# Order and spacing of the weight casts, and earlier splits and turns of two head pairs, in an attention and MLP kernel

## The chip, the cores and the metric

The kernel runs on one core of a Trainium2 chip. The metric is the device time of one execution in microseconds (us). The engines are named as the profile names them: PE is TensorE (PEld its weight loads), DVE is VectorE, ACT is ScalarE, POOL is GpSimd, SP is SyncE, which here only issues transfers. PEclk is the TensorE clock that was granted, as a share of full speed (in the row of slices, in tenths). "L247" is line 247 of the kernel.

## The reference

Eight batches of eight heads, 576 tokens by 64 columns each, go through an attention with a sharp threshold. The result x, 4608 tokens by 512, goes through two layers with h - tanh(h) between them.

```python
scores = scale * np.matmul(q, k.transpose(0, 1, 3, 2))
thresh = np.max(scores, axis=-1, keepdims=True) - tau
scores = np.where(scores >= thresh, scores, -1000000000.0)
scores = scores - np.max(scores, axis=-1, keepdims=True)
attn = np.exp(scores)
attn = attn / (np.sum(attn, axis=-1, keepdims=True) + 1e-09)
attn_out = np.matmul(attn, v)
...
h = x @ w_in            # 512 -> 2048
g = h - np.tanh(h)
return g @ w_out        # 2048 -> 512
```

Inputs and output are float32; q and k are cut on chip into a high and a low float16 part, so that the threshold falls where the reference has it.

## The kernel before

Heads go in pairs: 32 pairs p, four to a batch, nine query tiles to a pair. The program is one loop over *slots* s, one query tile each. In slot s it emits the scores of tile s+8, the shifted and bent scores z of tile s+5, the exponentials of tile s and the product with v of tile s-2. Pair p is therefore first touched in slot 9p - 8. What a pair needs ahead of that is put into slots by a plan: loads 16 to 14 slots before, the splits 8 and 7 before, and the *turns*, which transpose k and q.

```python
    PREP = (
        (LDK, lambda p: load(p, "k")),          # LDK = 16
        (LDK - 1, lambda p: load(p, "q")),
        (LDK - 2, lambda p: load(p, "v")),
        (8, lambda p: split(p, "k")),
        (7, lambda p: split(p, "q")),
        (5, lambda p: turn(p, "k")),
        (4, split_v),
    )
    plan = {}
    for p in range(1, NPAIR):
        first = TPP * p - AHEAD                 # 9 * p - 8
        for d, f in PREP[3 if p == 1 else 0 :]:
            d -= p == 1 and d in (3, 5)
            if d in (7, 8) and q_by_dma(p):
                d = d + 2
            if d == 5 and p >= 5:
                d = 6 if p % 2 else 3
            plan.setdefault(first - d, []).append(lambda p=p, f=f: f(p))
        d = 7 if q_by_dma(p) else 3 - (p == 1 or p % 2 == 0 or p >= 5)
        plan.setdefault(first - d, []).append(lambda p=p: turn(p, "q"))
```

A split is three GpSimd instructions. A turn is nine transposing matmuls on TensorE and a copy by VectorE; but for odd pairs from pair 9 on (and for pair 30), q is turned by one DMA transpose, issued from SP:

```python
    def q_by_dma(p):
        return p >= 2 * HPAIR and (p % 2 == 1 or p == 30)      # HPAIR = 4

    def turn(p, t):
        hl = hls.pop((p, t))
        if t == "q" and q_by_dma(p):
            m = mats[p, t] = qk_pool.tile([P, W], FP16, name=f"{t}T", tag=t)
            nc.sync.dma_start_transpose(                        # L247
                out=m.rearrange("p (c r) -> p c r", c=TPP),
                in_=hl.rearrange("p c a d -> p (c a d)"),
            )
            return
        ...
```

The tiles z of pairs 6 and up are also transposed by DMA from SP (L370), two tiles at a time, five slots before the exponential (L399) reads them. All loads go through SP too (L145 to L153 for q, k and v; L634 and L638 for weights), so one queue carries loads and both kinds of transposes in program order.

The weights of the two layers come in 16 pieces of 512 KB. Each is loaded as float32 into one of two staging buffers and cast to bfloat16 by GpSimd. Every slot in a list casts the piece loaded last and loads the next:

```python
    w_when = [4 * i + 3 for i in range(17)]
    ...
            if s + AHEAD in w_when:
                if loaded:
                    w_cast()            # GpSimd, L626
                piece = next(pieces, None)
                if piece:
                    w_load(piece)       # SP
```

The layers of batch b run in the slots of batch b+1. Batch 0 has none to run beside its attention: it is the *ramp*.

## Time and profile before

| | before |
|---|---|
| median of 3 runs | 533.77 us (532.88 to 534.11) |
| TensorE busy | 505.7 us, 95% of a span of 532.5 us |
| ScalarE, VectorE, GpSimd busy | 82%, 80%, 55% |
| first matmul of the hidden layer | 70.54 us after the start |

A line of a timeline gives the start and the duration in us, the engine, the line and operation, what it writes and reads, and in brackets how long its engine stood idle before it and who ended that. Here are two lines from much later, ScalarE's timeline in batch 1.

```profile
120.95 1.16 ACT L399 ACTIVATE pT<-zT 128x1152 f16<-128x1152 bf16 x1 [0.50 <-DMA zT<-z]
...
124.43 1.16 ACT L399 ACTIVATE pT<-zT 128x1152 f16<-128x1152 bf16 x1 [0.98 <-DMA zT<-z]
```

Both exponentials wait for a transposed z. They are the only waits of that kind worth naming in these 10 us, and together they are 1.5 us. So a DMA, not an engine, is already what arrives last at this place.

### The profile page before, as it was taken

What the parts mean: (1) busy time and instruction counts of PE and PEld (TensorE: products, weight loads), DVE (VectorE), ACT (ScalarE), POOL (GpSimd) and SP (SyncE); (2) the same over time, 40 slices, a digit from 0 to 9 for tenths busy, and PEclk for the clock granted to TensorE, in tenths of its full rate; (3) what the DMA queues carried; (4) which work ended last, traced back from release to release, by engine and by line L of the source; (5) the groups of instructions that cost most, each with busy time, mean ns of one, the idle gap of its engine ahead of it and who ended that gap; (6) DMA issues with size and microseconds to landing.
All of it is one profiled execution on the core that took longest, in us unless ns stands there. A gap on an engine that the chain in (4) does not pass through costs nothing.

```text
span 532.5 us, 12733 instructions
## 1 busy us (share of the span) xinstructions
PE 505.7 (95%) x4584; PEld 289.0 (54%) x4651; DVE 424.0 (80%) x1184; ACT 436.0 (82%) x617; POOL 290.3 (55%) x390
## 2 busy tenths in 40 slices
PE   7988899999999999999999999999999999999997
PEld 3666566555556555555555555656555555444444
DVE  5888878998988998898889898899889887554440
ACT  5999899998898998989888989898899899543330
POOL 7999987784745757475737474575747530000000
PEclk9999999999999999999999999999999999999999
DMA  6654556998997899899997989899989985301113
GB/s 199 188 185 148 160 173 179 207 154 192 180 194 150 186 178 214 169 174 202 179 198 142 211 173 201 155 189 187 205 170 178 197 156 110 105 21 40 39 41 79
DMA packets 202686, 85.31 MB, mean 160 GB/s; under 512 B 170240, under 2 KB 195072, under 8 KB 202624
## 3 DMA queue, kind: packets, MB, share of 16 engines
q1 hardware_dynamic: 202032, 84.08, 74.5%
q8 instruction: 36, 0.59, 0.5%
q10 hardware_dynamic: 592, 0.43, 0.3%
q14 instruction: 26, 0.21, 0.1%
HBM read 36.70 MB, written 9.44 MB: 87 GB/s over the span
## 4 chain that ended last, share of the span: by engine, by line
PE 62%; ACT 11%; POOL 9%; DVE 8%; issue 5%; DMA 4%; SPq 0%; POOLq 0%; ACTq 0%; DVEq 0%
PE psY L519 20%; PE psH L493 16%; PE psS L326 13%; ACT z L363 5%; DMA zT<-z 3%; PE psO L427 3%; ACT pT L399 3%; PE psHt L493 3%; DVE sc L336 3%; POOL kS L264 2%; ACT th L506 2%; DVE g L512 2%; PE ps_k L235 2%; PE psS L317 2%; POOL w_in_sb L626 1%
## 5 line engine op out<-in xcount | busy, mean ns | idle before, releaser
L336 DVE TENSOR_SCALAR_CACHE_REDUCE sc<-psS 128x576 f32<-128x576 f32 x288 | 214.3, 753 | 36.8 <-PE psS L326 22.8
L363 ACT ACTIVATE z<-sc,nb 128x576 bf16<-128x576 f32 x288 | 216.6, 770 | 29.2 <-DVE nb L348 27.1
L519 PE MATMUL psY<-w_out_sb,g 128*128 128x512 bf16 (+1 forms) x571 | 141.7, 373 | 2.4 <-issue 0.8
L264 POOL COPY kS<-kT 64x1152 f16<-64x1152 f16 x62 | 70.9, 1144 | 123.6 <-DVE nb L348 122.0
L399 ACT ACTIVATE pT<-zT 128x1152 f16<-128x1152 bf16 x117 | 135.0, 1154 | 3.7 <-DMA zT<-z 3.7
L493 PE MATMUL psH<-xT,w_in_sb 128*128 128x512 bf16 x436 | 114.1, 379 | 4.3 <-DVE g L512 2.3
L326 PE MATMUL psS<-kT,qT 128*128 128x512 f16 (+1 forms) x512 | 104.4, 285 | 4.6 <-DVE sc L336 2.1
L326 PEld LDWEIGHTS <-qT 128*128 128x128 f16 x1024 | 74.4, 97 | 59.9 <-issue 6.4
L512 DVE SCALAR_TENSOR_TENSOR g<-th,psH 128x512 bf16<-128x512 f32 x128 | 87.5, 684 | 20.4 <-ACT th L506 20.0
L326 PE MATMUL psS<-kS,qT 128*128 128x512 f16 x496 | 101.4, 286 | 0.3 <-POOL kS L264 0.3
L506 ACT ACTIVATE th<-psH 128x512 f32<-128x512 f32 x128 | 74.8, 584 | 23.4 <-PE psH L493 22.8
L519 PEld LDWEIGHTS <-g 128*128 128x128 bf16 x592 | 51.0, 98 | 56.8 <-issue 2.4
L493 PEld LDWEIGHTS <-w_in_sb 128*128 128x128 bf16 x576 | 49.1, 98 | 57.0 <-issue 4.7
L427 PE MATMUL psO<-vb,pT 128*128 128x65 bf16 x1024 | 53.3, 194 | 0.0
L427 PEld LDWEIGHTS <-pT 128*128 128x128 f16 x1024 | 44.2, 98 | 9.4
L188 POOL TENSOR_TENSOR qhl<-qraw,qhl 128x576 f16<-128x576 f32 x31 | 39.7, 1282 | 2.6
L188 POOL TENSOR_TENSOR khl<-kraw,khl 128x576 f16<-128x576 f32 x31 | 39.7, 1281 | 2.6
L391 ACT ACTIVATE pT<-psZ 128x512 f16<-128x512 bf16 (+1 forms) x54 | 35.1, 653 | 5.4 <-PE psZ L382 5.2
L532 DVE COPY yo<-psY 128x512 f32<-128x512 f32 (+1 forms) x31 | 21.1, 682 | 14.0 <-PE psY L519 12.4
L420 PE MATMUL psO<-vb,pT 128*128 128x130 bf16 x128 | 28.3, 221 | 1.8 <-ACT pT L399 1.1
L453 DVE TENSOR_TENSOR osb<-psO,rc 128x256 bf16<-128x256 f32 x64 | 27.2, 424 | 2.2
L258 DVE COPY kT<-ps_k 128x1152 f16<-128x1152 f16 x31 | 23.3, 752 | 5.8 <-PE ps_k L235 5.8
(79 smaller groups left out, 517.3 us busy)
## 6 DMA issues: line engine op xcount, KB each, us to landing
vraw<-in_v_dram SPq DMA_DIRECT2D x32, 256.0 KB, 3.9
out_dram<-yo SPq DMA_DIRECT2D x32, 256.0 KB, 3.1
kraw<-in_k_dram SPq DMA_DIRECT2D x31, 256.0 KB, 3.6
qraw<-in_q_dram SPq DMA_DIRECT2D x31, 256.0 KB, 3.7
wt<-in_moe_w_in_dram SPq DMA_DIRECT2D x8, 512.0 KB, 4.4
wt<-in_moe_w_out_dram SPq DMA_DIRECT2D x8, 512.0 KB, 4.3
zT<-z SPq DMA_TRANSPOSE x117, 3.5
kraw<-in_k_dram SPq DMA_DIRECT2D x32, 32.0 KB, 3.3
```

The costliest lines, as they stand in the source:

```text
L188: nc.gpsimd.tensor_tensor(out=hl[:, :, 1, :], in0=x, in1=hl[:, :, 0, :], op=ALU.subtract)
L264: nc.gpsimd.tensor_copy(out=o, in_=i)
L326: nc.tensor.matmul(out=ps[:, dst], lhsT=lhs, rhs=kk[:, src], start=(n == 0), stop=(n == 1),)
L336: nc.vector.tensor_scalar(out=sc, in0=ps[:, lo : lo + S], scalar1=SC, scalar2=None, op0=ALU.mult, op1=ALU.max, accum_out=mx[:, c : c + 1],)
L363: nc.scalar.activation(out=z, in_=sc, func=ACT.Prelu, bias=nb, scale=1.0, alpha=STEEP)
L391: nc.scalar.activation(out=pt[:, off * P : (off + n) * P], in_=ps[:, 0 : n * P], func=ACT.Exp)
L399: nc.scalar.activation(out=pt[:, 0 : n * P], in_=zts.pop(i)[:, 0:n, :], func=ACT.Exp)
L427: nc.tensor.matmul(out=po[:, t - 1 + ab, :], lhsT=pt[:, blk * P : (blk + 1) * P], rhs=vb[:, hh, c, :], start=False, stop=(n == 7), skip_gr ...
L493: nc.tensor.matmul(out=ps, lhsT=w_in_sb[:, c, n * P : (n + 1) * P], rhs=xs[m][:, c, :] if m < B else xR[:, c, :, :], start=(c == 0), stop= ...
L506: nc.scalar.activation(out=th, in_=ps, func=ACT.Tanh)
L512: nc.vector.scalar_tensor_tensor(out=gs[m][:, n, :], in0=th, scalar=-1.0, in1=ps, op0=ALU.mult, op1=ALU.add,)
L519: nc.tensor.matmul(out=ps, lhsT=gs[m][:, n, ms * P : (ms + 1) * P], rhs=w_out_sb[:, n, cols], start=(n == 0), stop=(n == DF_C - 1),)
```

## The change

The intent is to shorten the ramp, where GpSimd looks full. Casts leave it: the columns of the first eight hidden steps are cast first, and the other casts come later and at other distances. Pairs 2 and 4 split and turn k one slot sooner and turn q two slots sooner (4 slots ahead in place of 2).

```diff
-            for i in range(8):
+            for i in (0, 2, 4, 6, 1, 3, 5, 7) if w is moe_w_in else range(8):
                 yield flat, src, i, cols, w.shape[1]
...
-            if d == 5 and p >= 5:
+            if p in (2, 4):
+                d = {8: 9, 7: 8, 5: 6}.get(d, d)
+            elif d == 5 and p >= 5:
                 d = 6 if p % 2 else 3
...
-        d = 7 if q_by_dma(p) else 3 - (p == 1 or p % 2 == 0 or p >= 5)
+        d = 7 if q_by_dma(p) else 3 - (p == 1 or p >= 5)
+        d = 4 if p in (2, 4) else d
...
-    w_when = [4 * i + 3 for i in range(17)]
+    w_when = [3, 11, 19, 27] + [4 * i + 32 for i in range(4)] + [3 * i + 47 for i in range(9)]
```

Slots in this list count from -8, so the last second-layer cast moves from slot 59 to slot 63. A line added above moves the casts to L627.

## The prediction

> **What bounds the kernel now.** I read the page first. TensorE is busy 95% of the span at full clock, but its busy row is not even:
>
> ```profile
> ## 2 busy tenths in 40 slices
> PE   7988899999999999999999999999999999999997
> ...
> ACT  5999899998898998989888989898899899543330
> POOL 7999987784745757475737474575747530000000
> PEclk9999999999999999999999999999999999999999
> ```
>
> A slice is 13.3 us. From the third slice on the matrix work of the second layer fills TensorE's gaps. Only in the first five or six (to about 70 us: batch 0, four pairs of heads, no layer to fill in yet) does TensorE stand at 8 while GpSimd (POOL) stands at 9. That ramp is all that the change can shorten directly. Next, the busy time in stretches of 10 us:
>
> ```profile
> core 0: us, PE busy (x) PEld busy (x) DVE busy (x) ACT busy (x) POOL busy (x), PEclk, DMA share, GB/s
> ...
> 20.00:30.00 10.00, 8.77 (x122) 6.42 (x121) 8.68 (x26) 9.67 (x17) 9.53 (x11) 1.00 0.53 159
> 30.00:40.00 10.00, 8.71 (x123) 6.21 (x120) 8.71 (x29) 9.40 (x16) 9.47 (x13) 1.00 0.64 202
> 40.00:50.00 10.00, 9.27 (x135) 6.42 (x132) 8.34 (x27) 9.64 (x16) 9.45 (x13) 1.00 0.52 151
> 50.00:60.00 10.00, 8.08 (x113) 5.86 (x111) 8.51 (x29) 8.91 (x15) 9.47 (x13) 1.00 0.68 212
> 60.00:70.00 10.00, 8.37 (x98) 5.43 (x98) 8.69 (x28) 8.29 (x14) 9.56 (x12) 1.00 0.49 170
> ```
>
> The reader should see two engines full, not one. GpSimd never waits in its timeline from 10 us to 74 us (the 5% missing are the gaps between instructions), so it is a solid queue. ScalarE is at 94 to 97% from 20 to 50 us. So taking work off GpSimd gains only until ScalarE is at 100%: from 10 to 60 us ScalarE was busy 46.8 of 50 us, so 3.2 us is the most that stretch can give. The chain of work that ended last runs over GpSimd nearly without a break until 58 us, then turns to TensorE, VectorE and ScalarE:
>
> ```profile
> 33.62 1.28 POOL khl L188
> 34.90 0.98 POOL w_in_sb L626
> 35.88 0.65 POOL qraw L184
> 36.59 0.66 POOL qhl L187
> 37.34 1.28 POOL qhl L188
> ...
> 57.04 1.29 POOL khl L188
> 58.38 0.69 PE ps_k L235 x9
> 59.16 0.46 DVE kT L258
> ```
>
> I don't take that at its word: a chain can follow one engine back although another was nearly as full. So I asked whom GpSimd really kept waiting, in TensorE's and ScalarE's timelines:
>
> ```profile
> 38.67 0.68 PE L235 MATMUL ps_q<-ident_f,qhl 128*128 128x128 f16 x9 [0.77 <-POOL qhl L188]
> ...
> 58.38 0.68 PE L235 MATMUL ps_k<-ident_f,khl 128*128 128x128 f16 x9 [0.40 <-POOL khl L188]
> ```
>
> Only two of the eight turns of pairs 2 to 5 waited for GpSimd by more than 0.2 us (q of pair 3, k of pair 5). ScalarE's own gaps come in couples after each q turn, all put down to the transposed z: 0.33 and 0.26 us at 30 us (pair 2), 0.50 and 0.20 at 40 us (pair 3), 0.40 and 0.26 at 53 us (pair 4).
>
> **What the Trainium skill says.** "Perfetto Trace Analysis", section Tensor Engine Instruction, calls VectorE, ScalarE and GpSimd strict FIFOs; so a cast placed before a split delays that split by its whole length. The trace agrees: the 1.04 us cast at 34.84 us stands between the k and the q split of pair 3, and TensorE then waits 0.77 us for that q. "SBUF — State Buffer", section Who interferes with whom, says that a VectorE copy in a two-port mode and GpSimd block one another, so a moved cast might stretch. In this trace all 16 weight casts take 1037 to 1043 ns, beside whatever VectorE did, so I charge 1.04 us wherever they go. "DMA: Bandwidth & Descriptors", Anatomy of one DMA, says that a DMA's semaphore wait is served on the issuing sequencer before dispatch; so a transfer waiting for its buffer holds up those behind it. The trace shows the queue's records stretched where it waits: two second-layer loads from 73.28 us last 6.72 us. This matters for the loads that come at closer intervals.
>
> **The change, part by part.** No instruction is added or removed, in the weights or the pairs; the lists of both kernels show TensorE, VectorE, GpSimd and the load queue in another order.
>
> *Casts.* Before, the eight first-layer casts fall four slots apart and all eight lie on GpSimd by 55.6 us. After, the columns of the first eight hidden steps come first, at slots 3, 11, 19 and 24, the other half at 28, 32, 36 and 39; the eight second-layer casts follow every three slots from 42 to 63. Starts in GpSimd's timeline give the steps (start to start, from pair 2): split of k 2.74 us, of q 2.71, kS copies 2.40, split of v 1.27, a cast 1.01 to 1.04. Summed from 19.90 us in the new order, never waiting:
> k2 ends 22.6 (before 23.68), q2 25.35 (26.41), one cast, kS2, v2, then k3 32.7 (34.90), one cast, q3 36.5 (38.62), kS3, v3, k4 42.9 (47.1), one cast, q4 46.6 (49.84), kS4, v4, two casts, k5 55.0 (58.32).
> So q of pair 3 is ready 2.1 us sooner and k of pair 5 3.3 us sooner. Both exceed the waits of 0.77 and 0.40 us, so these two go, and GpSimd begins to idle, waiting for kT from VectorE. What follows in pair 3 is ScalarE's 0.50 + 0.20 us: I count 0.7. For pair 5, VectorE's copy waited 0.99 us for the turn, of which 0.40 is GpSimd's: I count 0.5.
>
> *Turns.* Pairs 2 and 4 split one slot sooner, turn k one sooner (5 to 4 before first use) and q two sooner (2 to 4). A turn takes one of the two large PSUM buffers that the scores rotate through, then 0.75 us of VectorE. At slot 8 the q turn of pair 2 met the normalization (0.19 + 0.42 + 0.34 us of VectorE, 26.88 to 27.79), and TensorE's next scores waited 0.72 us for VectorE. Moved to slot 6 it comes before that normalization. But the turn itself, its copy and the buffer it takes remain. For pair 2 it may also come too soon: k's slot is reached at about 22.3 us, its split done at 22.6. I count half of the ScalarE gaps of both pairs (0.59 + 0.66): 0.6.
>
> *Batch 1.* Three first-layer casts (slots 32, 36, 39) move past where they ended before, 3 x 1.04 = 3.1 us more on GpSimd after 60 us, and all second-layer casts come later. There GpSimd had slack: from 70 to 135 us it waited 13.6 us for VectorE and 2.3 us for one weight load. So most of it is hidden; for late splits I charge 0.3.
>
> Sum: -0.7 - 0.5 - 0.6 + 0.3 = -1.5 us. From 533.77 that is 532.3. I shade it to 532.2, since 3.2 us plus the gaps at 58 to 64 us is the ceiling, and the two parts may help one another.
>
> **The rivals.**
> (a) *ScalarE binds anyway.* It needs about 2.39 us for two tiles (two z at 0.67, pT 0.48 and 0.58 between starts), or 10.8 us for the nine tiles of a pair, against about 11.4 us that the ramp takes (22.9 us for slots 18 to 36). If its gaps come from the exchange of PSUM between TensorE and VectorE, GpSimd's relief buys nothing: 533.3 to 533.8. For it: six of the eight turns didn't wait for GpSimd. Against it: the largest single gap follows the wait for q of pair 3.
> (b) *GpSimd really sets the pace*, as the chain has it. Then 2 to 3.3 us come back: 530.3 to 531.7. For it: no wait in 64 us.
> (c) *Weight loads become the wait.* At three slots (about 3.9 us) a load that lands 4.3 us after issue (median) is late, and from slot 49 on the queue also carries transposes; one cast there already waited 2.29 us. Splits behind it would slip, and turns with them. Each exposed wait costs up to 1 to 2 us: 533 to 536. Against it: GpSimd idles about a third of 90 to 130 us, and an even pair's k split is five slots ahead of its turn.
> (d) *The lead is lost at batch 1*, where the layer's steps are tied to slots and ScalarE is again near full: 533.5.
>
> **Range and chances.** (a) and (b) bracket the sum, (c) gives the upper tail. The runs before spread over 532.88 to 534.11. I take 530.0 to 534.0. Two per cent would be 10.7 us; the ceiling of about 5 us (3.2 us, and 2.1 us of gaps at 58 to 64 us) excludes a gain of that size, and only several exposed load waits could cost as much: 0.01, 0.98, 0.01.
>
> **What would show each step.** The casts: GpSimd shows idle time between 30 and 60 us, and q of pair 3 and k of pair 5 no longer wait for it. The turns: ScalarE's gaps after the q turns of pairs 2 and 4 shrink, and TensorE's 0.72 us waits for VectorE there go. The net: the first matmul of the hidden layer, at 70.5 us now, starts 1 to 2 us sooner, and the end moves as much. Wrong would be: the hidden layer starts sooner but the end doesn't move (d); weight loads among GpSimd's waits with late turns after them (c); the same ScalarE gaps in spite of an idle GpSimd (a).

## The result, and the profile after

The changed kernel took 534.23 us in the median of 4 runs (533.60 to 534.88), against 533.71 us (532.88 to 534.11) for the kernel before in the same rounds. The ratio is 1.0012, with a 95% interval of 0.9993 to 1.003: the same time. Ratios here are the mean time of one kernel's fast runs over that of the other's of the same rounds, so not quite the ratio of the medians. The traced run of the changed kernel was its slowest, 534.88 us.

The page of the changed kernel shows where to look. Its rows in 40 slices of 13.3 us:

```profile
## 2 busy tenths in 40 slices
PE   7999899997999999999999999999999999999997
...
ACT  5999899987898998889888989899898999543330
POOL 7999987873755757475737574575747530000000
PEclk9999999998999999999999999999999999999999
```

The slices of the ramp rose for TensorE: 7 9 9 9 8 9 where they were 7 9 8 8 8 9. The tenth slice, 120 to 133 us, fell from 9 to 7, and the granted clock fell to 8 there. Busy sums don't tell this: TensorE's rose from 505.7 to 510.2 us, but the page counts 480 hidden matmuls where it counted 436, beside 576 weight loads of theirs in both: records are missing from both traces, and more from the earlier one.

The chain of waits, shares by engine, shows the intent fulfilled. First before, then after:

```profile
PE 62%; ACT 11%; POOL 9%; DVE 8%; issue 5%; DMA 4%; SPq 0%; POOLq 0%; ACTq 0%; DVEq 0%
```

```profile
PE 65%; ACT 15%; DVE 6%; issue 5%; POOL 4%; DMA 4%; SPq 0%; ACTq 0%; POOLq 0%; DVEq 0%
```

GpSimd's share fell from 9% to 4%, and the share of ScalarE grew. The stretches of 10 us, in the columns of the prediction, say the same of the ramp and show the hole after it:

```profile
30.00:40.00 10.00, 9.05 (x130) 6.39 (x127) 9.30 (x30) 9.85 (x17) 9.47 (x12) 1.00 0.57 162
40.00:50.00 10.00, 9.47 (x131) 6.69 (x128) 8.86 (x28) 9.80 (x17) 9.38 (x13) 1.00 0.25 84
...
120.00:130.00 10.00, 6.70 (x48) 3.70 (x49) 4.48 (x15) 7.19 (x9) 4.93 (x7) 0.83 0.98 197
```

In the ramp ScalarE went from 9.40 and 9.64 us to 9.85 and 9.80 of 10. In the hole TensorE is busy 6.70 us at a mean clock of 0.83, where before it read:

```profile
120.00:130.00 10.00, 9.22 (x89) 5.01 (x89) 8.24 (x26) 8.51 (x12) 4.96 (x8) 1.00 0.90 186
```

To follow the lead I read the same mark in both traces (the copy of x puts a pair's attention where the layers read it), as time after the start of GpSimd's first cast of v, since that cast starts anywhere from 8.4 to 9.6 us in the traces:

| mark | before | after | difference |
|---|---|---|---|
| first hidden matmul | 61.16 | 58.60 | -2.6 |
| copy of x of pair 6 (VectorE) | 104.20 | 102.18 | -2.0 |
| copy of x of pair 7 | 113.56 | 115.37 | +1.8 |
| copy of x of pair 8 | 131.84 | 133.47 | +1.6 |

The ramp gave 2.6 us, more than predicted. Then 3.8 us were lost between two marks 10 us apart. What happened there is one chain. GpSimd's timeline after:

```profile
110.10 1.04 POOL L627 CAST w_out_sb<-wt 128x1024 bf16<-128x1024 f32 x1 [1.99 <-DMA wt<-in_moe_w_out_dram]
...
112.59 1.28 POOL L188 TENSOR_TENSOR qhl<-qraw,qhl 128x576 f16<-128x576 f32 x1
```

The last weight cast waits 1.99 us for its load. Behind it stands the q split of pair 9, which ends at 113.87 us; before it ended at 113.03. So the split got later, although all else came sooner. Pair 9 is the first whose q is turned by DMA. SP's timeline, the issuing queue, after and then before:

```profile
113.90 1.28 SPq L247 DMA_TRANSPOSE qT<-qhl  x1
115.23 0.58 SPq L145 DMA_DIRECT2D kraw<-in_k_dram  x1
...
117.73 1.88 SPq L370 DMA_TRANSPOSE zT<-z  x1
```

```profile
113.06 1.28 SPq L247 DMA_TRANSPOSE qT<-qhl  x1
...
116.91 1.83 SPq L370 DMA_TRANSPOSE zT<-z  x1
```

The queue stands at L247 until the split is done. Behind it are the loads of k and q of pair 10 (four transfers, issued from 115.23 to 117.63 us), and behind those the z of slot 73. That z had been ready long before: in the order of the program it is the first of the two that ScalarE wrote from 112.08 us on. The chain in order of time, after:

```profile
116.85 0.89 ACT z L363 x2
117.73 4.24 DMA zT<-z
...
122.08 1.17 ACT pT L399
...
123.30 0.29 PE psO L420
```

The first line is worth a warning. The chain credits the z that ScalarE happened to finish at that moment, but the transfer was released by the queue in front of it. ScalarE pays, and TensorE's own timeline has a wait of 3.80 us for ScalarE in front of the "psO L420" of the chain, the product with v. ScalarE's own line is:

```profile
122.08 1.16 ACT L399 ACTIVATE pT<-zT 128x1152 f16<-128x1152 bf16 x1 [3.81 <-DMA zT<-z]
```

The sum closes. ScalarE was ready for this exponential at 118.27 us (122.08 less 3.81), before at 120.45 (120.95 less 0.50): it came 2.2 us sooner. The transposed z came 1.1 us later (ScalarE started at 122.08 against 120.95). 2.2 and 1.1 are the 3.3 us by which the wait grew. On the scale of the table it is 2.0 sooner and 1.3 later; of the 1.3, 1.0 was there when the transpose was issued, and the rest is its longer way. So the larger part of the wait is lead that could not be used. Slots 72 to 75 carry no work of the layers, so nothing filled the gap on TensorE, and its clock fell after it. Windows of 2 us, after:

```profile
120.00:122.00 2.00, 0.00 (x0) 0.00 (x0) 0.77 (x4) 0.00 (x0) 1.91 (x2) 1.00 0.96 216
...
124.00:126.00 2.00, 2.00 (x12) 1.00 (x10) 1.02 (x4) 1.84 (x3) 1.11 (x4) 0.50 1.07 191
```

Two microseconds with not one matmul, then 12 recorded matmuls at half clock where the kernel before has 20. The mean clock of the changed kernel's four runs was 0.995 to 0.997.

### The profile page after: what moved, and what is told of

Read it like the earlier page. It is cut to its first block, busy times and chain, and to the rows that moved or that the text cites. A ratio compares the mean times of both kernels' runs of the same rounds, so it can differ in the third digit from the quotient of the medians.

```text
span 533.1 us, 12805 instructions
## 1 busy us (share of the span) xinstructions
PE 510.2 (96%) x4651; PEld 289.7 (54%) x4651; DVE 423.6 (79%) x1184; ACT 435.9 (82%) x617; POOL 289.6 (54%) x390
## 4 chain that ended last, share of the span: by engine, by line
PE 65%; ACT 15%; DVE 6%; issue 5%; POOL 4%; DMA 4%; SPq 0%; ACTq 0%; POOLq 0%; DVEq 0%
PE psY L519 20%; PE psH L493 17%; PE psS L326 14%; ACT z L363 7%; ACT pT L399 4%; PE psO L427 3%; ACT pT L391 3%; PE psHt L493 3%; DMA zT<-z 2%; PE psS L317 2%; PE ps_k L235 2%; ACT th L506 2%; DVE sc L336 2%; DVE g L512 2%; DVE yo L532 1%
## 5 line engine op out<-in xcount | busy, mean ns | idle before, releaser
L519 PE MATMUL psY<-w_out_sb,g 128*128 128x512 bf16 (+1 forms) x592 | 145.9, 373 | 0.8 <-DVE yo L532 0.8
L493 PE MATMUL psH<-xT,w_in_sb 128*128 128x512 bf16 x480 | 124.0, 381 | 2.3 <-DVE g L512 2.3
L420 PE MATMUL psO<-vb,pT 128*128 128x130 bf16 x128 | 28.3, 221 | 4.5 <-ACT pT L399 4.0
```

Of the source, the lines that this page charges most:

```text
L493: nc.tensor.matmul(out=ps, lhsT=w_in_sb[:, c, n * P : (n + 1) * P], rhs=xs[m][:, c, :] if m < B else xR[:, c, :, :], start=(c == 0), stop= ...
L519: nc.tensor.matmul(out=ps, lhsT=gs[m][:, n, ms * P : (ms + 1) * P], rhs=w_out_sb[:, n, cols], start=(n == 0), stop=(n == DF_C - 1),)
```

## The experiments

Twelve kernels ran; each was compared with runs of the kernel before on the same chip. All gave correct results. The theory: the ramp gains what it should, and the lead is lost because the transposed z of slot 73 cannot come sooner, being tied to the q split of pair 9 and the loads in the one queue. The rivals: the late cast alone is the cause; the ramp part or the cast part is harmful by itself; the second-layer loads are too close; the DMA engines are full there, whatever the order.

| run | median us (range, runs) | ratio to before, 95% interval |
|---|---|---|
| e1 last cast later | 533.97 (533.47 to 535.04, 5) | 1.0005, 0.9993 to 1.0017 |
| e2 turns only | 533.70 (533.30 to 535.12, 5) | 1.0004, 0.9992 to 1.0016 |
| e3 casts only | 536.63 (534.54 to 537.62, 6) | 1.0048, 1.0032 to 1.0063 |
| e4 weight loads ahead | 533.19 (532.17 to 534.36, 6) | 0.9992, 0.9979 to 1.0004 |
| e5 pair 10 loads later | 531.76 (531.49 to 532.37, 5) | 0.9967, 0.9956 to 0.9979 |
| e6 loads and cast later | 530.82 (529.75 to 531.36, 5) | 0.9946, 0.9934 to 0.9958 |
| e7 before, loads later | 533.46 (531.90 to 533.81, 5) | 0.9993, 0.9981 to 1.0006 |
| e8 e6 with weight loads ahead | 532.50 (531.09 to 533.99, 6) | 0.9985, 0.9969 to 1.0001 |
| e9 casts only, no stall | 533.10 (532.34 to 533.45, 6) | 0.9974, 0.9959 to 0.9990 |
| e10 turns only, no stall | 533.59 (533.09 to 534.37, 6) | 0.9988, 0.9972 to 1.0004 |
| e11 casts only, second | 537.13 (1) | not timed in rounds |
| e12 loads three later | 530.41 (529.67 to 532.99, 6) | 0.9938, 0.9915 to 0.9961 |

The kernel before had medians of 533.78 (e1 to e4), 533.51 (e5 to e8), 534.28 (e9 to e11) and 534.14 us (e12), each of 11 runs.

### e1: the last weight cast after the q split of pair 9

```diff
-    ... + [3 * i + 47 for i in range(9)]
+    ... + [3 * i + 47 for i in range(8)] + [73]
```

> The changed kernel with its last second-layer cast two slots later (65 instead of 63), so that GpSimd splits the q of pair 9 before it. My theory: the lead of the ramp (2.2 to 2.7 us) is lost because this cast waits for its load (1.99 us) in front of that split, the DMA turn of q waits for the split in the load queue, and the transposes of z behind it come late, so that ScalarE waits 3.81 us and TensorE stands idle as long. Then the split ends about 3 us sooner (111 instead of 113.9 us), that wait of ScalarE falls below 1.5 us, and the run takes 530.5 to 531.8 us. Rival (the lead is lost at batch 1 anyhow, because another engine is full there): 533.3 to 534.5 us.

A miss. The late cast was indeed out of the way, and the turn of q came 2.8 us sooner. SP's timeline:

```profile
111.14 1.34 SPq L247 DMA_TRANSPOSE qT<-qhl  x1
...
115.03 1.83 SPq L370 DMA_TRANSPOSE zT<-z  x1
```

But the chain then holds "zT<-z" for 5.47 us, from 115.03 us, where it had 4.24: the transposed z landed at 120.50 us, only 1.5 us sooner. ScalarE waited 2.78 us and TensorE's clock fell to 0.50 again. So the cast is not the whole of the loss, and taking it away alone gained no time. The loads between the two transposes were still in front.

### e2 and e3: each part alone

e2 is the kernel before with the new turns of pairs 2 and 4; e3 is the changed kernel without them.

> Only the earlier splits and turns of pairs 2 and 4; the weights as before. Theory: the ramp gets 0.5 to 1.2 us shorter (first hidden matmul at 69.3 to 70.0 instead of 70.5 us), nothing in batch 1 changes, so 532.5 to 533.3 us. Rival (the turns brought the stall at 118 us): 534 us or more, with a wait of ScalarE for transposed z above 3 us.

The first hidden matmul came at 60.83 on the scale of the table of marks, 0.3 us sooner than before, and the time was that of before, above what I had expected. The turns came too soon for GpSimd, which still had all its casts in front:

```profile
23.09 0.68 PE L235 MATMUL ps_k<-ident_f,khl 128*128 128x128 f16 x9 [1.28 <-POOL khl L188]
```

TensorE waited 1.28 us for k of pair 2, 0.31 for q of pair 3 and 1.24 for q of pair 4.

The stall after 118 us is in the traced run, its slowest: ScalarE waited 2.01 us and TensorE 1.95, and the clock went to 0.50. The small lead does not explain it. On the scale of the marks ScalarE was ready 0.1 us sooner than before, and the transpose of z of slot 73 was issued 0.1 us sooner; but it landed 5.41 us after issue, where before no transpose of z issued from 110 to 124 us took more than 4.1. Why it took longer is open.

> Only the new order and times of the weights; the splits and turns as before. Theory: first hidden matmul at 68.3 to 69.5 us, and the same stall near 118 us, since the last casts stand where they do in the changed kernel; the stall eats whatever lead there is, so 533.7 to 534.7 us. Rival (the turns brought the stall): 532.0 to 532.8 us and no wait of ScalarE for transposed z above 1.5 us.

The first hidden matmul came at 59.99, 1.2 us sooner, yet the kernel is 0.48% slower: above what I had expected. Its traced run, the fastest of the six at 534.54 us, showed a wait of 2.72 us for z, which cannot stand for the slow ones; that is what e11 was run for. With the turns the lead was 2.6 us, though apart the parts give 0.3 and 1.2: they help one another in the ramp. The traces show by which wait: of the three largest waits for splits that e2 has (1.28, 0.31 and 1.24 us), the changed kernel keeps 0.29 us of the first and nothing of the others. Fewer casts stand in front of its splits.

### e4: second-layer loads one piece further ahead

```diff
-    wt_pool = pool("wt", 2)
+    wt_pool = pool("wt", 3)
...
-                piece = next(pieces, None)
-                if piece:
-                    w_load(piece)
+                for _ in range(2 if s + AHEAD == 47 else 1):
+                    piece = next(pieces, None)
+                    if piece:
+                        w_load(piece)
```

> The changed kernel with three staging buffers for weights and every second-layer load issued one period sooner; the casts stay in their places on GpSimd. If the late landing of the loads is what holds the split (theory, first form), GpSimd's waits for weight loads (6.4 us in three) go, the q split of pair 9 ends near 112 us, and the run takes 531 to 532.2 us. If the mere place of the last cast before the split is enough (second form: 1.0 us of it), the gain stays below 0.8 us: 533.3 to 534.2 us.

GpSimd no longer waits for any weight load, and L247 is issued at 111.03 us, as in e1. The z of slot 73 is issued at 114.88 and takes 5.47 us again, and ScalarE waits 2.76. So two ways to free the split end in the same wait, which speaks for the loads of pair 10 in the queue. The time, 533.19 us, is not clear of that of the kernel before (0.9992). Rival (c) of the prediction names something true but not the last thing.

This run also shows what the clock does, since its trace has the wait without the fall. Matmuls of the hidden layer just after the wait, in e1 (four in 1.89 us) and in e4 (four in 1.03 us):

```profile
123.01 1.89 PE L493 MATMUL psH<-xT,w_in_sb 128*128 128x512 bf16 x4
```

```profile
122.73 1.03 PE L493 MATMUL psH<-xT,w_in_sb 128*128 128x512 bf16 x4
```

From the product with v after the wait to the next one, the same instructions take TensorE 4.96 us in e1 (121.82 to 126.78) and 3.28 us in e4 (121.67 to 124.95): the lower clock costs 1.7 us there. What of it reaches the end is not shown. From the copy of x of pair 7 to that of pair 8 e1 took 18.65 us and e4 17.17, but the kernel before took 18.28 at full clock and the changed kernel 18.10 with the fall. Nor do the times of e4 settle it: two runs at a mean clock of 0.996 took 533.93 and 534.36 us, three at 0.999 took 532.17 to 532.65, and one at 1.000 took 533.73.

### e5, e6 and e7: the loads of pair 10 out of the way

The loads of pair 10 are put five slots later, behind the z transposes that matter. e5 does this to the changed kernel, e6 to e1, e7 to the kernel before.

```diff
         for d, f in PREP[3 if p == 1 else 0 :]:
             d -= p == 1 and d in (3, 5)
+            d -= 5 * (p == 10 and d >= LDK - 2)
```

> The changed kernel, with the loads of k, q and v of pair 10 five slots later, so that in the load queue the two transposes of z after the DMA turn of q of pair 9 come before them. Run e1 put the split earlier and the transposed z still landed at 120.5 us, behind these loads (issued 115.03, landing 5.5 us). Theory now: two things hold that transpose, the turn's wait for the split (113.9 us) and the loads behind it (about 2.5 us of issue, and their bytes). Here only the second goes: ScalarE's wait of 3.81 us falls to 0.8 to 2 us; 531.5 to 533.2 us. Rival (the landing is late because the DMA engines are full there, whatever the order): a wait above 3 us and 533.8 us or more.

> Run e1 (last cast behind the split of q of pair 9) with the loads of pair 10 five slots later as well. Theory: the transpose of z is issued near 112.5 us and lands by 117 us; ScalarE waits less than 0.7 us; TensorE's idle stretch and the lower granted clock after it go (0.997 to 0.999 or more); 530.3 to 531.8 us. Rival (full DMA engines): a wait above 2 us and 533.3 us or more.

> The kernel before with the loads of pair 10 five slots later. Its own waits for transposed z there are 0.50 and 0.98 us. If the loads are what makes them, they go and it takes 532.4 to 533.3 us; a gain as large as in the changed kernel (2 us or more) would say that the change itself brings nothing.

e5 took 531.76 us: the wait of 3.81 us was gone (the exponential after it waited 0.39), the clock stayed at 1.00, and the lead of 2.2 us was still there at pair 8 (129.63 against 131.84). e6 took 530.82 us, with no wait at this place. Its queue, and the exponential of slot 73:

```profile
111.38 1.32 SPq L247 DMA_TRANSPOSE qT<-qhl  x1
112.80 3.53 SPq L370 DMA_TRANSPOSE zT<-z  x2
116.38 0.58 SPq L145 DMA_DIRECT2D kraw<-in_k_dram  x1
```

```profile
117.95 1.15 ACT L399 ACTIVATE pT<-zT 128x1152 f16<-128x1152 bf16 x1
```

The transposes now follow L247 at once and the loads follow them. This answers the rival of full DMA engines as far as it said that the order would not matter. But the loads were also moved out of the time in which the transpose runs, so how much was waiting in the queue and how much was sharing of the DMA engines is not told apart. e7 is the control: the same shift of loads is worth nothing in the kernel before (533.46 us, 0.9993), which has no lead to keep. Its two waits of 0.50 and 0.98 us went, and one of 2.41 us came at 137.73.

So the gain of e6 is the gain of the change, kept. e6 over e7, both with the loads moved, is 0.9946 / 0.9993 = 0.9953, which is 2.5 us of 533.5 (about 1.6 to 3.4 us by the two intervals): within noise the lead at the first hidden matmul, 2.6 us. At the copy of x of pair 8 it is 2.4 us (129.40 against 131.84). With the loads moved, the later cast is worth 0.9946 / 0.9967, about 1.1 us, though alone (e1) it was worth nothing: the two stood one behind the other.

e6 beats both kernels. It is not free of the same trouble: the later loads reach GpSimd late (4.88 us of waiting for k of pair 10), and ScalarE waits 2.21 us for a transposed z at 134.67 us.

### e8: all three at once

e8 is e6 with the edit of e4.

> Run e6 with three staging buffers and every second-layer load a period sooner (as in e4). GpSimd's waits for weight loads are gone, so splits and the DMA turn come as early as ScalarE lets them; theory 530.0 to 531.5 us, at most 0.5 us better than e6 since these waits no longer end a chain there. If the waits of GpSimd for loads still matter beside the order of the queue, it is 1 us or more better than e6.

A miss: 532.50 us, slower than e6, and spread over 2.9 us. The traced run was its fastest, 531.09 us, at a clock of 1.00, and shows nothing that e6 doesn't; other runs had a mean clock down to 0.996, so some of them probably fell into a wait that this trace doesn't have. Why is open. Loading the weights further ahead puts yet more into the same queue at that time, but that is argued, not shown.

### e9 and e10: each part alone, without the stall

e9 is e3 with the shifts of e6; e10 is e2 with the shift of the loads.

> Run e6 (no stall) with the splits and turns of pairs 2 and 4 back where they were: what the weights alone are worth. In run e3 the first hidden matmul came at 69.1 us (before 70.5, changed kernel 67.8). Theory: the lead now reaches the end, so about 1.4 us below the kernel before: 531.7 to 532.5 us, 1.0 to 1.6 us above e6. Rival (the turns are needed for any gain, as the slow runs of e3 could say): 533.3 us or more.

> Run e7 (the kernel before with the loads of pair 10 later) with the earlier splits and turns of pairs 2 and 4: what the turns alone are worth. In run e2 the first hidden matmul came at 69.6 us. Theory: 0.9 us below e7 or the kernel before: 532.2 to 532.9 us. Rival (an earlier turn is worth nothing by itself): as e7, 533.2 us or more.

The casts alone are then worth 0.26% (1.4 us), where with the stall they lost 0.48%. The turns alone give 0.12% (0.6 us), with an interval that includes no gain. In microseconds both medians lie above what I had expected (the kernel before stood at 534.28 on that chip), and that of e10 is what the rival foretold: alone the turns are worth nothing that can be told from noise. The leads at the first hidden matmul repeat those of e3 and e2: 59.98 and 60.92. This rules out the rival that the cast part is harmful in itself: only its meeting with the queue, and with the last cast, was.

### e11: the casts alone once more

The kernel of e3 unchanged, run for a trace of a slow run.

> Run e3 once more, for a second trace: its runs went from 534.5 to 537.6 us and the traced one was the fastest. If a slow one is caught, theory: the time is in the stall after 118 us (idle TensorE of 3 us or more, then a lower granted clock), up to 3 us more of it than in the first trace; rival: it is spread over the later batches, and the landmarks up to 160 us are as in the first trace.

It took 537.13 us and shows the same place, only worse. ScalarE's timeline:

```profile
123.07 1.16 ACT L399 ACTIVATE pT<-zT 128x1152 f16<-128x1152 bf16 x1 [4.58 <-DMA zT<-z]
```

TensorE then ran 7 recorded matmuls in the 2 us from 126 us on, at a clock of 0.50. The copy of x of pair 6 was at 103.25, 1.0 us ahead of before; that of pair 7 at 117.16, 3.6 us behind. At the copy of x of pair 8 it stands 3.0 us behind the trace of e3 (136.17 against 133.18), and the two runs differ by 2.6 us. So this slow run is the same stall with more idle time and a longer half clock, as expected.

### e12: the loads three slots later

e6 with 3 in place of 5, to spare GpSimd's late k.

> Run e6 with the loads of pair 10 three slots later instead of five: only one transpose of z (that of tile 73, the one that was late) goes ahead of them. In e6 GpSimd waited 4.88 us for the k of pair 10 and ScalarE 2.21 us for transposed z at 134.7 us. If this late load is what feeds that wait, both shrink by 1.5 us or more and the run takes 530.0 to 530.8 us; the transpose of tile 73 stays in time (no wait of ScalarE above 0.7 us at 118 us). Rival: nothing on the path, 530.6 to 531.3 us as e6.

530.41 us. GpSimd's wait for k of pair 10 went from 4.88 to 1.88 us, and ScalarE's wait for z at 134 us from 2.21 to 1.47, but two small waits for z came before it (0.44 and 0.69 us). Its interval overlaps that of e6: the two aren't told apart, and the place of these loads is a range, not a point.

## Why the prediction was wrong

Predicted were 532.2 us and 530.0 to 534.0; the median was 534.23, 0.23 us outside the range on the slow side, which is less than the spread of its own four runs (533.60 to 534.88). So the miss of the range is slight; the miss of the mechanism is not. "Within 2%" held.

**The step that failed** is "the first matmul of the hidden layer [...] starts 1 to 2 us sooner, and the end moves as much", with "for late splits I charge 0.3". The matmul started 2.6 us sooner, the end did not move, and 3.8 us of lead were lost between the copies of x of pairs 6 and 7, in the wait for one transposed z. e5 and e6, which take the loads (and the last cast) out of its way, make the end move.

**Casts.** The sum was right: -1.2 us, measured -1.2 at the first hidden matmul with the casts alone (e3, e9). That is partly luck. At the copies of x of pairs 1 and 2 the lead of e3 is 0.4 us, where the gaps of pair 3 were to give 0.7; the stage of pair 5 gave 0.8, where 0.5 was counted. The two errors cancel. As predicted, the waits for q of pair 3 and k of pair 5 are gone. One sign I named was wrong: GpSimd did not begin "to idle, waiting for kT"; it stays as full to 72 us as before, because the next splits simply start sooner.

**Turns.** I counted -0.6. TensorE's waits of 0.72 us for VectorE after the q turns of pairs 2 and 4 are gone (0.22 us is left for pair 4), and ScalarE's gaps after the q turns of pairs 2, 3 and 4 shrank from 1.95 us (0.33, 0.26, 0.50, 0.20, 0.40, 0.26) to a single one of 0.20. Alone the turns moved the first hidden matmul by only 0.2 to 0.3 us (e10, e2), but in company with the casts the two moved it 2.6. My "the two parts may help one another" was right and its size was missed: 1.8 us counted, 2.6 measured. "For pair 2 it may also come too soon" was right too, above all without the casts moved (e2). As foreseen for pair 2, TensorE waited a little (0.29 and 0.26 us) for GpSimd at the earlier turns.

**Batch 1.** "So most of it is hidden; for late splits I charge 0.3" was too little: behind the late split the transpose of z was issued 1.0 us later than before. I had summed GpSimd's slack over 65 us (13.6 us of waiting) and taken a sum for a guarantee at every slot. Rival (c) was put off with "an even pair's k split is five slots ahead of its turn". That holds for even pairs; the split that was hit is the q of pair 9, an odd one, two slots ahead of a turn that is a DMA and stands at the head of an in-order queue.

But the late split is not the main loss: e1, which takes it away, gained no time.

**The larger omission** is that I credited the lead to the end without looking where it must be cashed. The trace before had ScalarE waiting 0.50 and 0.98 us for a transposed z at 121 and 124 us. An engine that waits there has no use for arriving sooner, unless the DMA arrives sooner as well, and that DMA was tied to a GpSimd split which the same change put behind one more cast. Rival (d), the lead lost in batch 1, was right in outcome (533.5) and wrong in its reason: neither the slots of the layers nor a full ScalarE held it, as e6 shows, which keeps the lead with both unchanged.

**The lower clock** I did not consider. It costs 1.7 us of TensorE's time just after the wait (e1 against e4); what it costs at the end is not shown.

**What stays open** is why a transpose of z takes 4.0 to 5.5 us at this place in one trace or another, and so why the runs of one kernel differ (e3, e8).

**The skill's rule.** The strict FIFO of "Perfetto Trace Analysis" (Tensor Engine Instruction), which the prediction used for the ramp, was the very rule that hit pair 9: its split ended 3.77 us after the start of the cast in front (110.10 to 113.87), on top of that cast's wait of 1.99.

## What to carry to other kernels

Before a shortened stage is credited to the total, go to the next place with a wait and ask which wait ends last there, and whether its whole chain moves with the lead; a wait of half a microsecond for a DMA in the old trace can mean that there is no room. When loads with slack share an in-order queue with transposes that have none, place the loads behind them. And slack summed over a long window says nothing about the one slot in which an instruction is due.

## What the Trainium skill lacked or had wrong

- "TensorE: Matmul & The Clock Gate", Part 1 (The HAM clock gate): it gives half clock "after ≥1 idle window (~3.4µs)". Here the clock fell to 0.50 after TensorE had stood idle in one piece for only 1.95 us (e2) and 2.76 us (e1), while after 2.71 us (e4) it stayed at 1.00. In the 4 us from 118 to 122 TensorE was busy 1.22 us in e1 and 1.27 us in e4, so the two can't be told apart by that either. An idle time shorter than the stated window can be enough, and need not be. The page also says that the window is free-running and the effect run-variable, and this agrees.
- "DMA: Bandwidth & Descriptors", Queues, rings and completion order: it says that descriptors are consumed in ring order on each DMA engine, and gives no figure for what a transpose on chip pays behind ordinary loads of the same queue. Here it took 4.24 us and 5.47 us (changed kernel, e1) from issue to landing with the loads of pair 10 just in front, against a median of 3.5 us over all transposes of z. The order does not set it alone: in e5, with these loads behind, one took 5.04 us.
- None of the pages looked up says that loads and transposes which share one issuing engine should be ordered by how soon they are due. It decided this case: 3.3 us of longer wait in the changed kernel, and about 3.1 us of gain when the loads of pair 10 were moved (e6 against e1, 0.9946 / 1.0005).
